# Loading the values of pairs 5 to 8 through GpSimd's software DMA queue, in bf16

## The chip, the cores and the metric

The kernel runs on one core of a Trainium2 chip. Its engines work side by side, each in the order of its own queue: TensorE (PE, matrix products), VectorE (DVE), ScalarE (ACT), GpSimd (POOL) and SyncE (SP, which here only issues DMAs). Sixteen DMA engines carry data between HBM and the on-chip memories, whoever issued the transfer. The metric is the device time of one execution in microseconds (us), lower being better.

## What is computed

A gated linear attention with a complex decay, then a normalised feed-forward layer. Cut to what matters:

```python
# q, k, v, a_re, a_im: (4 batches, 8 heads, 768 steps, 48)
for t in range(S):
    S_re, S_im = ar * S_re - ai * S_im, ar * S_im + ai * S_re   # a, capped at |a| = 0.999
    S_re = S_re + outer(k[:, :, t], v[:, :, t])
    y[:, :, t] = q[:, :, t] @ S_re
x = y, heads side by side                                        # (4, 768, 384)
xn = (x - mean) / sqrt(var + 1e-6) * g_ln
out = x + relu(xn @ w_ch1) @ w_ch2                               # 384 -> 1536 -> 384
```

All inputs and the output are float32.

## The kernel before

The steps of time are cut into chunks of 128. Two chunks make a pair; a batch has three pairs, and the four batches give pairs 0 to 11 (so chunks 0 to 23, chunks 2P and 2P+1 being those of pair P). Per pair the kernel works out the running log magnitude and phase of the decay (`ln`, `iv`, `r`, `r2`, `u`, `l`, `lc`, `th` on the gates, `dec` and `ph` as matmuls with triangular matrices, then `e`, `en`, `sin`, `cos`), scales the keys and queries by them (`ke`, `qe`, then `ks`, `qs`, each with a cosine half `.0` and a sine half `.1`), and transposes these per chunk (`kT`/`ksT`, `qT`/`qsT`: by PE and a copy, or by a DMA transpose issued from SP). Per chunk n, `am.n` is the product of keys and queries, `atm.n` its masked copy, `gm.n` adds keys times values to the state, `G.n` copies the state out, `y.n` is `atm` times values plus queries times state, `x.n` its copy, `bn.n` its mean and variance, and `xtr`/`xT` its transpose. Per pair follow the feed-forward products `mm1`, `relu`, `mm2`, the scale `rstd`, the sum `ot` and the store `st`.

Nothing of the order is left to a scheduler. A long text, `PLAN`, lists every step as `name:engine`, with a digit for the PSUM bank. Each engine executes its steps in the order in which they stand there. A suffix `@other` makes a step wait until another has ended, which the author uses to let DVE and POOL take turns. Buffers are rings of a few tiles (`RINGS`): 2 for `vf`, 4 for `v`, 3 for `k`, `q`, `ks` and `qs`.

The change concerns the values. For each pair P, `vf.P.0` and `vf.P.1` (L403) load the two chunks as float32 from HBM into the tile `vf`, 128 partitions by 8 heads by 48 numbers each, issued by SP. `v.P` (L411 on ACT, L413 on DVE or POOL) then casts the whole pair, 128 x 768, to bf16 into the tile `v`, which the matmuls of `gm` (L643) and `y` (L665) read. The plan puts `v.5` on DVE, `v.6` and `v.8` on POOL and `v.7` on ACT. The weights are loaded by POOL's software queue (`wl`, L363 and L365), which casts them from float32 to bf16 on the way.

The loads issued from SP wait in SP's queue with the DMA transposes (L597), the loads of gates, keys and queries (L444, L403) and the stores (L760), in the plan's order.

Of the kernel before, what the change touches and what calls it, by code (L numbers as in the profile page):

```python
# [24 lines left out]
RINGS = {"are": 3, "aim": 3, "q": 3, "k": 3, "vf": 2, "v": 4, "w": 2, "r": 3, "r2": 2, "l": 3,  # L25
# [6 lines left out]


QUARTER = {0, 1, 2, 3}

ENGINES = {"P": "PE", "A": "ACT", "V": "DVE", "G": "POOL", "S": "SP"}

# [41 lines left out]
am.7:P2 r2.5.0:A xT.4:V7 q.5.0:S xtr.5:P0 decc.4:V6 am.6:P4 r.6.0:G ot.3:V1 xT.5:A0 ph.5.0:P6 cos.4.0:A  # L79
vf.4.1:S atm.6:V4 mm1.2.1.1:P0 sin.5.0:A6 are.7.0:S ke.4.0.0:G atm.7:V2 y.6:P4 mm1.2.1.0:P0 abs.5.0:A6  # L80
ke.4.0.1:G gm.6:P5 x.6:A4 are.8.0:S mm1.2.2.0:P2 G.6:V5 cos.5.0:A qe.4.0.1:G xtr.6:P4 relu.2.1:V0 y.7:P6
gm.7:P5 q.5.1:S ks.4.0.1:G x.7:A6 mm1.2.2.1:P2 bn.4:V r2.6.0:A xtr.7:P0 mm1.2.0.1:P6 vf.5.0:S xT.7:V0
relu.2.2:A2 xT.6:V4 mm1.2.0.0:P6 qs.4.0.0:G G.7:V5 st.1:S th.6.0:A bn.7:V mm1.3.0.0:P0 k.5.0:S relu.2.0:V6
mm1.3.1.0:P2 ks.4.0.0:G aim.7.0:S mm1.3.2.1:P4 bn.5:V mm1.3.2.0:P4 tab.log.8:A u.5.0:A bn.6:V rstd.2:G
mm1.3.1.1:P2 u.6.0:A qs.4.0.1:V mm2.5.0:P6 l.5.0:V relu.3.2:A4 qsT.9:S mm2.4.0:P7 mm1.3.0.1:P0 lc.5.0:V
relu.3.1:A2 l.6.0:V ksT.8:S mm2.4.1:P7 ln.7.0:A relu.3.0:V0 dec.5.0:P4 vf.5.1:S mm2.4.2:P7 e.5.0:A4 q.6.1:S
lc.6.0:V v.4:V mm2.5.1:P6 en.5.0:A4 st.3:S qe.5.0.1:V dec.6.0:P2 ot.4:V7 k.5.1:S iv.7.0:A mm2.6.0:P0 en.6.0:A2
r.7.0:G k.6.1:S qT.8:P1 kT.9:P7 ln.8.0:A qsT.8:V1 mm2.5.2:P6 aim.8.0:S e.6.0:A2 ksT.9:V7 am.8:P4 qe.5.0.0:G
r2.7.0:A mm2.7.0:P1 atm.8:V4 st.4:S gm.8:P7 rstd.3:A qs.5.0.0:G st.2:S am.9:P2 u.7.0:A G.8:V7 aim.9.0:S
mm2.6.1:P0 atm.9:V2 ph.6.0:P4 ke.5.0.0:G k.6.0:S qs.5.0.1:V y.9:P2 tab.trig.9:A th.7.0:A gm.9:P7 l.7.0:V  # L90
y.8:P3 q.6.0:S mm2.7.1:P1 abs.6.0:A4 x.9:V2 ke.5.0.1:G@l.7.0 mm2.6.2:P0 are.9.0:S car.6.0:A4 G.9:V7 sin.6.0:A4
mm2.7.2:P1 x.8:V3 qe.6.0.1:V oa.6:A0 qT.11:P7 vf.6.0:S bn.8:V xtr.8:P2 xtr.9:P3 ph.7.0:P4 lc.7.0:V xT.9:A3
q.7.1:S xT.8:V2 cos.6.0:A ks.5.0.0:V mm1.4.1.1:P2 abs.7.0:V4 vf.6.1:S ke.6.0.1:G@ks.5.0.0 car.7.0:A4
mm1.4.1.0:P2 sin.7.0:A4 ks.5.0.1:V dps.6:P0 qsT.10:S oa.7:A1 v.5:V mm1.4.0.1:P4 relu.4.1:A2 ke.6.0.0:V
mm1.4.0.0:P4 qsT.11:V7 ot.6:G@ke.6.0.0 k.7.1:S kT.11:P1 relu.4.0:V4 mm1.4.2.0:P2 ks.6.0.0:G k.7.0:S
mm1.4.2.1:P2 decc.6:V0 tab.log.10:A ln.9.0:A ksT.11:V1 mm2.8.0:P7 q.7.0:S relu.4.2:A2 ot.5:V6 qe.6.0.0:G
kT.10:P0 bn.9:V am.11:P4 k.8.1:S iv.8.0:A qs.6.0.0:G mm2.9.0:P6 ksT.10:V0 rstd.4:A st.6:S dec.7.0:P2 atm.11:V4
# [2 lines left out]
th.9.0:A y.11:P1 kT.12:P2 ke.7.0.1:G th.8.0:A x.11:V1 q.8.0:S y.10:P3 qsT.13:V0 ksT.12:A2 xtr.11:P1 ks.7.0.1:G  # L100
ph.8.0:P4 x.10:V3 cos.7.0:A xT.11:V1 xtr.10:P0 ph.9.0:P2 abs.8.0:V4 xT.10:A0 ks.7.0.0:G ot.8:V7 mm1.5.0.1:P0
sin.9.0:A2 ot.9:V6 st.8:S mm1.5.0.0:P0 car.9.0:A2 q.8.1:S abs.9.0:V2 ot.7:G sin.8.0:A4 mm1.5.1.0:P6 are.10.0:S
relu.5.0:V0 vf.7.0:S mm1.5.1.1:P6 r2.8.0:A qe.7.0.1:G mm1.5.2.1:P2 cos.8.0:A qe.7.0.0:G are.11.0:S relu.5.1:V6
am.12:P4 r2.9.0:A mm1.5.2.0:P2 v.6:G atm.12:V4 st.9:S am.13:P0 qs.7.0.0:G vf.7.1:S mm2.10.0:P6 atm.13:V0
mm2.11.0:P7 tab.log.12:A u.8.0:A st.7:S y.12:P4 qs.7.0.1:G gm.12:P5 aim.10.0:S x.12:V4 mm2.10.1:P6 G.12:A5
bn.10:V relu.5.2:A2 mm2.11.1:P7 l.8.0:V ksT.15:S y.13:P0 u.9.0:A mm2.10.2:P6 lc.8.0:V x.13:A0 xtr.12:P1
bn.11:V gm.13:P5 k.9.1:S xT.12:A1 dec.8.0:P2 l.9.0:V rstd.5:G xtr.13:P0 dps.7:P4 en.8.0:A2 ksT.14:S
mm2.11.2:P7 xT.13:V0 G.13:V5 e.8.0:A2 ke.8.0.0:G@l.9.0 mm1.6.0.1:P0 ot.11:V7 ln.11.0:A vf.8.0:S mm1.6.2.1:P2
lc.9.0:V decc.7:V4 ln.10.0:A ke.8.0.1:G@lc.9.0 mm1.6.2.0:P2 vf.8.1:S v.7:A mm1.6.1.0:P4 ks.8.0.0:V aim.11.0:S
qT.15:P7 iv.10.0:A qe.8.0.1:G@ks.8.0.0 mm1.6.0.0:P0 qsT.15:V7 relu.6.2:A2 qe.8.0.0:G mm1.6.1.1:P4 ot.10:V6  # L110
vf.9.0:S relu.6.0:A0 gm.14:P7 bn.12:V r.10.0:G am.15:P2 k.9.0:S qT.14:P6 relu.6.1:A4 atm.15:V2 mm2.12.0:P0
qsT.14:A6 mm2.13.0:P1 qs.8.0.1:V dec.9.0:P4 G.14:V7 r2.10.0:V am.14:P2 qs.8.0.0:V mm2.12.1:P0 u.10.0:A
# [1 line left out]
gm.15:P7 ksT.17:S x.14:V2 xtr.15:P6 qT.16:P3 e.9.0:A4 G.15:V7 ke.9.0.1:G xtr.14:P2 mm2.13.2:P1 r.11.0:V  # L114
xT.14:A2 q.9.0:S mm2.12.2:P0 rstd.6:G xT.15:A6 ksT.16:S mm1.7.0.0:P4 ke.9.0.0:G@r.11.0 ot.12:V0 mm1.7.0.1:P4
qsT.16:V3 st.12:S tab.trig.13:A cos.9.0:A mm1.7.1.1:P6 st.11:S bn.15:V q.9.1:S mm1.7.2.0:P2 th.10.0:A l.10.0:V
vf.9.1:S mm1.7.2.1:P2 relu.7.0:A4 lc.10.0:V st.10:S mm1.7.1.0:P6 bn.14:V v.8:G@lc.10.0 relu.7.2:A2 k.10.0:S
dps.9:P0 ks.9.0.1:V mm2.15.0:P4 relu.7.1:A6 q.10.0:S decc.9:V0 am.17:P2 qe.9.0.0:V gm.16:P0 r2.11.0:A
atm.17:V2 ks.9.0.0:G@qe.9.0.0 q.10.1:S am.16:P6 mm2.15.1:P4 th.11.0:A G.16:V0 mm2.14.0:P5 atm.16:V6 v.9:G
ksT.18:S dec.10.0:P2 qe.9.0.1:G y.17:P0 ot.13:V1 tab.log.14:A u.11.0:A y.16:P6 k.11.0:S x.17:V0 mm2.14.1:P5  # L120
# [32 lines left out]
class Graph:  # L153
# [59 lines left out]
def kernel(  # L213
# [54 lines left out]
    def T(name, i):  # L268
        return tiles[name][i % RINGS[name]]
# [69 lines left out]
    def c_mask():  # L339
# [11 lines left out]
          needs=["ue"])  # L351
    for i in range(RINGS["car"]):
        g.add(f"car0.{i}", lambda i=i: nc.gpsimd.memset(tiles["car"][i], WINDOW),
                  needs=["ue"])
# [7 lines left out]
    for i in range(NG):  # L362
        g.add(f"wl.{i}", lambda i=i: nc.gpsimd.dma_start(  # L363
            out=w1b[:, :, ts(i, 512)], in_=moe_w_ch1.rearrange("(dc p) j -> p dc j", p=C)[:, :, ts(i, 512)]))
        g.add(f"wl.{NG + i}", lambda i=i: nc.gpsimd.dma_start(  # L365
            out=w2b[:, ts(i, JG)], in_=moe_w_ch2.rearrange("(jc p) e -> p jc e", p=C)[:, ts(i, JG)]))
# [11 lines left out]
    for jb in range(NG):  # L378
# [7 lines left out]
        for ec in range(ND):  # L386
            g.add(f"wc.{jb}.{ec}", lambda jb=jb, ec=ec, o=o: nc.vector.scalar_tensor_tensor(
                out=w1b[:, ec, ts(jb, 512)], in0=w1b[:, ec, ts(jb, 512)], scalar=gln[:, ds(ec, 1)],
# [3 lines left out]
    def pair_ops(P):  # L392
        b, pp = divmod(P, PB)
# [5 lines left out]
        add = g.add  # L399

        for c in range(R):
            for nm, ap in (("k", k), ("q", q), ("vf", v)):
                add(f"{nm}.{P}.{c}", lambda nm=nm, ap=ap, c=c: nc.sync.dma_start(  # L403
                    out=T(nm, P)[:, c],
                    in_=ap[b].rearrange("h (c p) d -> p c h d", p=C)[:, pp * R + c]),
                    uses=[(nm, P)])

        def f_v():
# [3 lines left out]
            else:  # L412
                {"DVE": nc.vector, "POOL": nc.gpsimd}[eng(nm)].tensor_scalar(  # L413
                    out=T("v", P), in0=T("vf", P), scalar1=1.0, scalar2=0.0, op0=ALU.mult,
                    op1=ALU.add)
        add(f"v.{P}", f_v, needs=[f"vf.{P}.0", f"vf.{P}.1"], uses=[("vf", P), ("v", P)])


        for i in range(NS):
# [23 lines left out]
            for nm, ap in (("are", a_re), ("aim", a_im)):  # L443
                add(f"{nm}.{X}", lambda nm=nm, ap=ap, hs=hs: nc.sync.dma_start(  # L444
                    out=T(nm, P)[:, hs], in_=ap[b][hs].rearrange(
                        "h (k p j) d -> p k h (j d)", p=C, j=R)[:, pp]), uses=[(nm, P)])
            add(f"ln.{X}", lambda S_=S_: act(out=S_("w"), in_=S_("are"), func=AF.Ln),  # L447
                needs=[f"are.{X}"], uses=[("are", P), ("w", P)])
            add(f"iv.{X}", lambda S_=S_: act(out=S_("are"), in_=S_("w"), func=AF.Exp, scale=-1.0),  # L449
                needs=[f"ln.{X}"], uses=[("are", P), ("w", P)])  # L450
            add(f"r.{X}", lambda S_=S_, X=X: tt(f"r.{X}", out=S_("r"), in0=S_("aim"), in1=S_("are"),
                                                op=ALU.mult),
                needs=[f"iv.{X}", f"aim.{X}"], uses=[("are", P), ("aim", P), ("r", P)])

            def f_r2(S_=S_, X=X):
# [6 lines left out]
                needs=[f"r2.{X}", "one"], uses=[("r2", P)])  # L462

            def f_l(S_=S_):
# [4 lines left out]
                out=S_("l"), in0=S_("l"), scalar1=LNCAP, scalar2=LNEPS, op0=ALU.min, op1=ALU.add),  # L469
                needs=[f"l.{X}"], uses=[("l", P)])  # L470
# [8 lines left out]
            for nm, sc in (("en", -1.0), ("e", 1.0)):  # L479
                add(f"{nm}.{X}", lambda nm=nm, sc=sc, X=X, fs=fs, view=view: act(  # L480
                    out=T(nm, P)[:, :, fs], in_=view(f"dec.{X}"), func=AF.Exp, scale=sc),
                    needs=[f"dec.{X}"], uses=[(nm, P)], ps=(f"dec.{X}", nb))

            add(f"th.{X}", lambda S_=S_: act(out=S_("th"), in_=S_("r"), func=AF.Arctan),
                needs=[f"r.{X}"], uses=[("r", P), ("th", P)])

            def f_ph(X=X, fs=fs, view=view, step=step):
# [12 lines left out]
                uses=[("th", P), ("car", P)], ps=(f"ph.{X}", nb))  # L500

            if not last:
                def f_car(X=X, fs=fs, v16=v16):
# [7 lines left out]
                    uses=[("car", P + 1)], ps=(f"ph.{X}", nb))  # L511
# [3 lines left out]
                needs=[f"ph.{X}"], uses=[("trig", P)], ps=(f"ph.{X}", nb))  # L515
# [48 lines left out]
        def stack(nm):  # L564
            return [f"{nm}.{P}.{i}.{a}" for i in range(NS) for a in range(2)]
# [19 lines left out]
        for c in range(R):  # L585
# [49 lines left out]
            if not (last and c == R - 1):  # L635
                def f_gm(n, c, nfirst):
                    ps = bank(f"gm.{P}")[:, 0:DM]
                    if c == 0 and not nfirst:
                        nc.tensor.matmul(ps, lhsT=ident,
                                         rhs=T("G", n - 1).rearrange("p h d -> p (h d)"),  # L640
                                         start=True, stop=True, skip_group_check=True)
                    for h in range(H):
                        nc.tensor.matmul(heads(ps)[:, h], lhsT=T("ks", P)[:, c, h],  # L643
                                         rhs=T("v", P)[:, c, h], start=nfirst, stop=True,
                                         skip_group_check=True)
                was = [] if nfirst else [f"G.{n - 1}"]
                add(f"gm.{n}", lambda n=n, c=c, nfirst=nfirst: f_gm(n, c, nfirst),
                    needs=stack("ks") + [f"v.{P}", f"pad.ks.{P % RINGS['ks']}"] + was,
                    uses=[("ks", P), ("v", P)] + ([("G", n - 1)] if was and c == 0 else []),
                    ps=(f"gm.{P}", 1))  # L650
                if c == 0:
                    add(f"G.{n}", lambda n=n: put(f"G.{n}", T("G", n),
                                                  heads(bank(f"gm.{P}")[:, 0:DM])),
                        needs=[f"gm.{n}"], uses=[("G", n)], ps=(f"gm.{P}", 1))
                else:
                    add(f"G.{n}", lambda n=n: tt(
                        f"G.{n}", out=T("G", n), in0=heads(bank(f"gm.{P}")[:, 0:DM]),
                        in1=T("dec", P).unsqueeze(2).to_broadcast([C, H, D]), op=ALU.mult),
                        needs=[f"gm.{n}", f"decc.{P}"], uses=[("G", n), ("dec", P)],
                        ps=(f"gm.{P}", 1))  # L660

            def f_y(n, c, nfirst):
# [143 lines left out]
```

## Time and profile before

The kernel took 193.36 us, the median of three runs (191.88, 193.36, 194.04). The profiled execution took 192.54 us, of which the profile's span is 190.8.

| what | value |
|---|---|
| PE busy | 174.8 us (92%), 2061 matmuls |
| DVE, ACT busy | 154.8 us (81%), 157.3 us (82%) |
| POOL busy | 109.9 us (58%), without its DMA issues |
| hardware DMA queue (SP) | 126960 packets, 34.09 MB, 86.2% of 16 engines |
| software DMA queue (POOL) | 2784 packets, 2.36 MB, 8.3% of 16 engines |
| loads of `vf` | 24 of 192 KB, median 4.2 us from issue to landing (3.3 to 10.9) |
| casts `v` | 7 on POOL (median 834 ns), 4 on DVE (552 ns), 1 on ACT (830 ns) |

Times in views of the trace are microseconds from the span's start. A line of the timeline gives the start, the time, the engine, the source line, the operation with output and input tiles, the count, and in square brackets how long the engine stood idle before it and what ended that. DMA packets here are runs of contiguous bytes: a chunk of values has 128 x 8 runs of 48 float32 numbers, 192 B each. The share of a queue can add up to more than 100% with others, since packets of several transfers are under way in one engine at once.

### The profile page before, as it was taken

To read this page: it belongs to the slowest core of one execution; us is meant where nothing else is said; L and a number is where in the kernel's file an instruction comes from. 1 tells how busy PE (TensorE), PEld (TensorE's weight loads), DVE (VectorE), ACT (ScalarE), POOL (GpSimd) and SP (SyncE) were. 2 spreads that over 40 slices of the span, in tenths; PEclk is the share of its full clock that TensorE was granted. 3 is DMA by queue.
4 is the path that set the end of the run, shared out by engine and by line. 5 is a ranking of instruction groups with operands and counts; after the bars stand their busy time and mean duration, and the time that the engine had idled before them with its cause. 6 is when DMAs were issued, how large, how long until landed. Compare 5 with 4: busy or idle time off the path is not lost.

```text
span 190.8 us, 5173 instructions
## 1 busy us (share of the span) xinstructions
PE 174.8 (92%) x2061; PEld 134.5 (70%) x2061; DVE 154.8 (81%) x283; ACT 157.3 (82%) x217; POOL 109.9 (58%) x128
## 2 busy tenths in 40 slices
PE   5758777999999999999899999999999999999990
PEld 4646455986868889676687786877768777886760
DVE  0397879998979999969979899798998898596422
ACT  4798998999898999999799898979996976283450
POOL 7505297599508999175291995758292756630030
PEclk9978999999999999999999999999999999999998
DMA  5999999899999999699989999987999999995132
GB/s 140 290 226 220 204 207 192 204 193 200 203 240 201 228 236 219 115 221 255 246 147 240 150 241 272 188 190 144 227 205 145 185 186 172 239 121 164 45 124 84
DMA packets 129768, 36.78 MB, mean 193 GB/s; under 512 B 123984, under 2 KB 129744, under 8 KB 129744
## 3 DMA queue, kind: packets, MB, share of 16 engines
q1 hardware_dynamic: 126960, 34.09, 86.2%
q0 software_dynamic: 2784, 2.36, 8.3%
q8 instruction: 16, 0.26, 0.6%
q14 instruction: 8, 0.07, 0.1%
HBM read 28.31 MB, written 4.72 MB: 173 GB/s over the span
## 4 chain that ended last, share of the span: by engine, by line
PE 50%; DMA 15%; DVE 9%; ACT 6%; POOL 6%; SPq 6%; issue 4%; POOLq 0%; DVEq 0%; ACTq 0%
PE banks L740 17%; PE banks L719 14%; DMA aim<-in_a_im_dram 5%; DMA w2b<-in_moe_w_ch_dram 4%; PE banks L592 4%; SPq L403 3%; PE banks L615 3%; PE banks L495 3%; DMA are<-in_a_re_dram 2%; PE banks L476 2%; DMA qsT<-qs 2%; DVE atm L291 2%; DMA q<-in_q_dram 2%; POOL r L291 2%; PE banks L665 2%
## 5 line engine op out<-in xcount | busy, mean ns | idle before, releaser
L740 PE MATMUL banks<-w2b,h 128*128 128x384 bf16 x288 | 55.3, 326 | 0.3 <-DMA w2b<-in_moe_w_ch_dram 0.3
L719 PE MATMUL banks<-xT,w1b 128*128 128x256 bf16 x432 | 51.3, 273 | 0.9 <-ACT trig L513 0.9
L719 PEld LDWEIGHTS <-w1b 128*128 128x128 bf16 x432 | 41.4, 98 | 7.3 <-issue 0.8
L740 PEld LDWEIGHTS <-h 128*128 128x128 bf16 x288 | 25.8, 97 | 13.5 <-issue 0.4
L291 DVE TENSOR_TENSOR atm<-banks,mask 128x1024 bf16<-128x1024 f32 x24 | 28.8, 1218 | 3.6 <-PE banks L615 3.5
L730 ACT ACTIVATE h<-banks 128x1024 bf16<-128x1024 f32 x26 | 26.0, 1019 | 5.7 <-PE banks L719 4.4
L291 POOL TENSOR_TENSOR ke<-k,en 128x384 bf16<-128x384 f32 x19 | 17.2, 916 | 16.8 <-DVE qs L291 5.8
L774 ACT ACT_TABLE_LOAD x19 | 24.4, 1283 | 1.1 <-PEq L790 0.8
L291 POOL TENSOR_TENSOR ks<-ke,trig 128x768 bf16<-128x768 bf16 (+1 forms) x12 | 18.9, 1583 | 6.6 <-DVE qs L291 2.0
L752 POOL TENSOR_TENSOR ot<-ot,x 128x384 f32<-128x384 f32 x7 | 6.4, 916 | 18.2 <-ACT ot L745 15.9
L291 POOL TENSOR_TENSOR qs<-qe,trig 128x768 bf16<-128x768 bf16 (+1 forms) x10 | 15.7, 1569 | 0.3
L754 DVE SCALAR_TENSOR_TENSOR ot<-banks,rstd,x 128x384 f32<-128x384 f32 x17 | 10.3, 610 | 6.8 <-ACT h L730 3.5
L615 PE MATMUL banks<-qsT,ksT 128*128 128x128 bf16 x192 | 14.6, 219 | 1.1 <-DVE ksT L288 0.9
L291 POOL TENSOR_TENSOR qe<-q,e 128x384 bf16<-128x384 f32 x14 | 12.7, 918 | 4.2 <-ACT trig L513 3.4
L615 PEld LDWEIGHTS <-ksT 128*128 128x128 bf16 x192 | 12.0, 98 | 3.2 <-DVE ksT L288 1.0
L291 POOL TENSOR_TENSOR r<-aim,are 128x768 f16<-128x768 f32 x6 | 10.9, 1816 | 5.5 <-ACT are L449 5.4
L476 PE MATMUL banks<-l,u_e 128*128 128x384 f16 (+1 forms) x52 | 10.9, 342 | 3.5 <-DVE l L468 3.4
L732 DVE TENSOR_SCALAR h<-banks 128x1024 bf16<-128x1024 f32 x10 | 12.1, 1216 | 2.0 <-PE banks L719 2.0
L678 DVE BATCH_NORM_STATS2 stats<-x 128x6 f32<-128x384 bf16 x24 | 13.1, 547 | 0.0
L769 PE MATMUL banks<-u_e 128*128 128x256 f16 x72 | 11.1, 312 | 2.2 <-POOL u_e L325 2.2
L447 ACT ACTIVATE w<-are 128x768 f32<-128x768 f32 (+1 forms) x13 | 10.1, 794 | 3.4 <-DMA are<-in_a_re_dram 3.3
L665 PE MATMUL banks<-v,atm 128*128 128x48 bf16 x192 | 12.1, 183 | 0.1
(95 smaller groups left out, 383.7 us busy)
## 6 DMA issues: line engine op xcount, KB each, us to landing
k<-in_k_dram SPq DMA_DIRECT2D x24, 192.0 KB, 4.0
q<-in_q_dram SPq DMA_DIRECT2D x24, 192.0 KB, 4.3
vf<-in_v_dram SPq DMA_DIRECT2D x24, 192.0 KB, 4.2
out_dram<-ot SPq DMA_DIRECT2D x24, 192.0 KB, 2.9
are<-in_a_re_dram SPq DMA_DIRECT2D x11, 384.0 KB, 4.6
aim<-in_a_im_dram SPq DMA_DIRECT2D x11, 384.0 KB, 5.0
w1b<-in_moe_w_ch_dram POOLq DMA_DIRECT2D x3, 384.0 KB, 7.0
w2b<-in_moe_w_ch_dram POOLq DMA_DIRECT2D x3, 384.0 KB, 7.7
```

The source lines that it names most:

```text
L291: {"DVE": nc.vector, "POOL": nc.gpsimd}[eng(name)].tensor_tensor(**kw)
L476: nc.tensor.matmul(heads(ps[:, c]), lhsT=u_e[:, c, j], rhs=step(T("l", P), j), start=(j == 0), stop=(j == R - 1))
L615: nc.tensor.matmul(ps[:, h], lhsT=T("ksT", n)[:, h], rhs=T("qsT", n)[:, h], start=True, stop=True)
L665: nc.tensor.matmul(ps[:, h], lhsT=T("atm", n)[:, h], rhs=T("v", P)[:, c, h], start=True, stop=nfirst)
L678: nc.vector.bn_stats(out=T("stats", n), in_=T("x", n))
L719: nc.tensor.matmul(ps[:, jj], lhsT=w1b[:, dc, ts(gi * JG + jj, C)], rhs=T("xT", P)[:, dc].rearrange("p c t -> p (c t)"), start=(dc == 0), ...
L730: act(out=dst, in_=src, func=AF.Relu)
L732: nc.vector.tensor_scalar(out=dst, in0=src, scalar1=0.0, scalar2=None, op0=ALU.max)
L740: nc.tensor.matmul(bank(f"o.{n}")[:, 0:DM], lhsT=T("h", P)[:, j, ts(c, C)], rhs=w2b[:, j], start=(j == 0), stop=(j == NJ - 1))
L754: nc.vector.scalar_tensor_tensor(out=T("ot", n), in0=bank(f"o.{n}")[:, 0:DM], scalar=T("rstd", P)[:, ds(c, 1)], in1=T("x", n), op0=ALU.mul ...
L769: g.add(f"warm.{i}", lambda i=i: nc.tensor.matmul(bank(f"warm.{i}")[:, 0:256], lhsT=u_e[:, 0, 0], rhs=u_e[:, 1].rearrange("p j t -> p (j t ...
L774: g.add(f"tab.{nm}.{i}", lambda tab=tab: nc.scalar.preload_act_table_set(tab))
```

## The change

For pairs 5 to 8 the loads of the values are issued by POOL instead of SP. They write straight into the bf16 tile `v`; the DMA converts. The casts `v.5` to `v.8` go, and so does these pairs' use of `vf`. In the plan each `vf.P.c` keeps its place in the text, with the engine changed from S to G, so that it now stands in POOL's queue between the POOL steps that surround it there. The matmuls of `gm` and `y` wait for the two loads instead of the cast.

```diff
+CAST = {5, 6, 7, 8}
...
             for nm, ap in (("k", k), ("q", q), ("vf", v)):
+                if nm == "vf" and P in CAST:
+                    add(f"vf.{P}.{c}", lambda c=c: nc.gpsimd.dma_start(
+                        out=T("v", P)[:, c],
+                        in_=v[b].rearrange("h (c p) d -> p c h d", p=C)[:, pp * R + c]),
+                        uses=[("v", P)])
+                    continue
                 add(f"{nm}.{P}.{c}", lambda nm=nm, ap=ap, c=c: nc.sync.dma_start(
...
-        add(f"v.{P}", f_v, needs=[f"vf.{P}.0", f"vf.{P}.1"], uses=[("vf", P), ("v", P)])
+        if P not in CAST:
+            add(f"v.{P}", f_v, needs=[f"vf.{P}.0", f"vf.{P}.1"], uses=[("vf", P), ("v", P)])
+        values = [f"v.{P}"] if P not in CAST else [f"vf.{P}.{c}" for c in range(R)]
...
-                    needs=stack("ks") + [f"v.{P}", f"pad.ks.{P % RINGS['ks']}"] + was,
+                    needs=stack("ks") + values + [f"pad.ks.{P % RINGS['ks']}"] + was,
...
-                needs=[f"atm.{n}", f"v.{P}"] + ([] if nfirst else [f"G.{n - 1}", f"qsT.{n}"]),
+                needs=[f"atm.{n}"] + values + ([] if nfirst else [f"G.{n - 1}", f"qsT.{n}"]),
```

In the plan, `vf.5.0` to `vf.8.1` change from `:S` to `:G`, and `v.5:V`, `v.6:G`, `v.7:A` and `v.8:G@lc.10.0` are taken out. POOL's queue around the new issues then reads as follows (an excerpt, POOL's steps alone):

```
ks.4.0.1  vf.5.0  qs.4.0.0  ks.4.0.0  rstd.2  vf.5.1  r.7.0
ke.5.0.1@l.7.0  vf.6.0  vf.6.1  ke.6.0.1@ks.5.0.0
ot.7  vf.7.0  qe.7.0.1  qe.7.0.0  qs.7.0.0  vf.7.1  qs.7.0.1  rstd.5
ke.8.0.0@l.9.0  vf.8.0  ke.8.0.1@lc.9.0  vf.8.1  qe.8.0.1@ks.8.0.0  qe.8.0.0  r.10.0
```

More of the change, by code (lines that the diff above doesn't have):

```diff
@@ L81 @@
 ke.4.0.1:G gm.6:P5 x.6:A4 are.8.0:S mm1.2.2.0:P2 G.6:V5 cos.5.0:A qe.4.0.1:G xtr.6:P4 relu.2.1:V0 y.7:P6
-gm.7:P5 q.5.1:S ks.4.0.1:G x.7:A6 mm1.2.2.1:P2 bn.4:V r2.6.0:A xtr.7:P0 mm1.2.0.1:P6 vf.5.0:S xT.7:V0
+gm.7:P5 q.5.1:S ks.4.0.1:G x.7:A6 mm1.2.2.1:P2 bn.4:V r2.6.0:A xtr.7:P0 mm1.2.0.1:P6 vf.5.0:G xT.7:V0
 relu.2.2:A2 xT.6:V4 mm1.2.0.0:P6 qs.4.0.0:G G.7:V5 st.1:S th.6.0:A bn.7:V mm1.3.0.0:P0 k.5.0:S relu.2.0:V6
@@ L85 @@
 mm1.3.1.1:P2 u.6.0:A qs.4.0.1:V mm2.5.0:P6 l.5.0:V relu.3.2:A4 qsT.9:S mm2.4.0:P7 mm1.3.0.1:P0 lc.5.0:V
-relu.3.1:A2 l.6.0:V ksT.8:S mm2.4.1:P7 ln.7.0:A relu.3.0:V0 dec.5.0:P4 vf.5.1:S mm2.4.2:P7 e.5.0:A4 q.6.1:S
+relu.3.1:A2 l.6.0:V ksT.8:S mm2.4.1:P7 ln.7.0:A relu.3.0:V0 dec.5.0:P4 vf.5.1:G mm2.4.2:P7 e.5.0:A4 q.6.1:S
 lc.6.0:V v.4:V mm2.5.1:P6 en.5.0:A4 st.3:S qe.5.0.1:V dec.6.0:P2 ot.4:V7 k.5.1:S iv.7.0:A mm2.6.0:P0 en.6.0:A2
@@ L91 @@
 y.8:P3 q.6.0:S mm2.7.1:P1 abs.6.0:A4 x.9:V2 ke.5.0.1:G@l.7.0 mm2.6.2:P0 are.9.0:S car.6.0:A4 G.9:V7 sin.6.0:A4
-mm2.7.2:P1 x.8:V3 qe.6.0.1:V oa.6:A0 qT.11:P7 vf.6.0:S bn.8:V xtr.8:P2 xtr.9:P3 ph.7.0:P4 lc.7.0:V xT.9:A3
-q.7.1:S xT.8:V2 cos.6.0:A ks.5.0.0:V mm1.4.1.1:P2 abs.7.0:V4 vf.6.1:S ke.6.0.1:G@ks.5.0.0 car.7.0:A4
-mm1.4.1.0:P2 sin.7.0:A4 ks.5.0.1:V dps.6:P0 qsT.10:S oa.7:A1 v.5:V mm1.4.0.1:P4 relu.4.1:A2 ke.6.0.0:V
+mm2.7.2:P1 x.8:V3 qe.6.0.1:V oa.6:A0 qT.11:P7 vf.6.0:G bn.8:V xtr.8:P2 xtr.9:P3 ph.7.0:P4 lc.7.0:V xT.9:A3
+q.7.1:S xT.8:V2 cos.6.0:A ks.5.0.0:V mm1.4.1.1:P2 abs.7.0:V4 vf.6.1:G ke.6.0.1:G@ks.5.0.0 car.7.0:A4
+mm1.4.1.0:P2 sin.7.0:A4 ks.5.0.1:V dps.6:P0 qsT.10:S oa.7:A1
+mm1.4.0.1:P4 relu.4.1:A2 ke.6.0.0:V
 mm1.4.0.0:P4 qsT.11:V7 ot.6:G@ke.6.0.0 k.7.1:S kT.11:P1 relu.4.0:V4 mm1.4.2.0:P2 ks.6.0.0:G k.7.0:S
@@ L102 @@
 sin.9.0:A2 ot.9:V6 st.8:S mm1.5.0.0:P0 car.9.0:A2 q.8.1:S abs.9.0:V2 ot.7:G sin.8.0:A4 mm1.5.1.0:P6 are.10.0:S
-relu.5.0:V0 vf.7.0:S mm1.5.1.1:P6 r2.8.0:A qe.7.0.1:G mm1.5.2.1:P2 cos.8.0:A qe.7.0.0:G are.11.0:S relu.5.1:V6
-am.12:P4 r2.9.0:A mm1.5.2.0:P2 v.6:G atm.12:V4 st.9:S am.13:P0 qs.7.0.0:G vf.7.1:S mm2.10.0:P6 atm.13:V0
+relu.5.0:V0 vf.7.0:G mm1.5.1.1:P6 r2.8.0:A qe.7.0.1:G mm1.5.2.1:P2 cos.8.0:A qe.7.0.0:G are.11.0:S relu.5.1:V6
+am.12:P4 r2.9.0:A mm1.5.2.0:P2
+atm.12:V4 st.9:S am.13:P0 qs.7.0.0:G vf.7.1:G mm2.10.0:P6 atm.13:V0
 mm2.11.0:P7 tab.log.12:A u.8.0:A st.7:S y.12:P4 qs.7.0.1:G gm.12:P5 aim.10.0:S x.12:V4 mm2.10.1:P6 G.12:A5
@@ L107 @@
 bn.11:V gm.13:P5 k.9.1:S xT.12:A1 dec.8.0:P2 l.9.0:V rstd.5:G xtr.13:P0 dps.7:P4 en.8.0:A2 ksT.14:S
-mm2.11.2:P7 xT.13:V0 G.13:V5 e.8.0:A2 ke.8.0.0:G@l.9.0 mm1.6.0.1:P0 ot.11:V7 ln.11.0:A vf.8.0:S mm1.6.2.1:P2
-lc.9.0:V decc.7:V4 ln.10.0:A ke.8.0.1:G@lc.9.0 mm1.6.2.0:P2 vf.8.1:S v.7:A mm1.6.1.0:P4 ks.8.0.0:V aim.11.0:S
+mm2.11.2:P7 xT.13:V0 G.13:V5 e.8.0:A2 ke.8.0.0:G@l.9.0 mm1.6.0.1:P0 ot.11:V7 ln.11.0:A vf.8.0:G mm1.6.2.1:P2
+lc.9.0:V decc.7:V4 ln.10.0:A ke.8.0.1:G@lc.9.0 mm1.6.2.0:P2 vf.8.1:G
+mm1.6.1.0:P4 ks.8.0.0:V aim.11.0:S
 qT.15:P7 iv.10.0:A qe.8.0.1:G@ks.8.0.0 mm1.6.0.0:P0 qsT.15:V7 relu.6.2:A2 qe.8.0.0:G mm1.6.1.1:P4 ot.10:V6
@@ L116 @@
 qsT.16:V3 st.12:S tab.trig.13:A cos.9.0:A mm1.7.1.1:P6 st.11:S bn.15:V q.9.1:S mm1.7.2.0:P2 th.10.0:A l.10.0:V
-vf.9.1:S mm1.7.2.1:P2 relu.7.0:A4 lc.10.0:V st.10:S mm1.7.1.0:P6 bn.14:V v.8:G@lc.10.0 relu.7.2:A2 k.10.0:S
+vf.9.1:S mm1.7.2.1:P2 relu.7.0:A4 lc.10.0:V st.10:S mm1.7.1.0:P6 bn.14:V
+relu.7.2:A2 k.10.0:S
 dps.9:P0 ks.9.0.1:V mm2.15.0:P4 relu.7.1:A6 q.10.0:S decc.9:V0 am.17:P2 qe.9.0.0:V gm.16:P0 r2.11.0:A
```

## The prediction

> **What bounds the kernel now.** I read the busy table of the page first, then busy time by stretches, then TensorE's (PE's) instructions in order, then the queue that the change loads (GpSimd, POOL) with the vector engine (DVE) beside it. The page, engine by engine, in 40 slices of 4.77 us:
>
> ```profile
> PE   5758777999999999999899999999999999999990
> DVE  0397879998979999969979899798998898596422
> ACT  4798998999898999999799898979996976283450
> POOL 7505297599508999175291995758292756630030
> PEclk9978999999999999999999999999999999999998
> ```
>
> From slice 9 (43 us) to slice 36 PE is full and its granted clock is full; DVE and ScalarE (ACT) are nearly so. Busy time by stretches (columns: window, length, busy us and count of PE, PEld, DVE, ACT, POOL, clock, DMA share, GB/s), for those the change touches last:
>
> ```profile
> 104.00:116.00 12.00, 12.00 (x150) 9.50 (x148) 11.44 (x16) 11.45 (x16) 11.63 (x10) 1.00 1.10 211
> 116.00:128.00 12.00, 11.95 (x152) 9.49 (x151) 10.51 (x23) 10.26 (x15) 6.93 (x8) 1.00 1.18 218
> ```
>
> A busy PE could still be a waiting PE, so I looked at when its matmuls start:
>
> ```profile
> 119.44 2.78 PE L719 MATMUL banks<-xT,w1b 128*128 128x256 bf16 x24
> 122.06 0.61 PE L592 MATMUL banks<-ident,qs 128*128 128x128 bf16 x8
> 122.51 1.47 PE L719 MATMUL banks<-xT,w1b 128*128 128x256 bf16 x12
> 123.82 0.33 PE L639 MATMUL banks<-G,ident 128*128 128x384 bf16 x1
> 123.98 0.36 PE L643 MATMUL banks<-v,ks 128*128 128x48 bf16 x8
> ```
>
> 24 matmuls of 256 columns go from 119.44 to 122.06, 109 ns each; the 12 after 122.51 take 109 ns each again (1.31 / 12). In the same way 384 columns take 163 ns, 128 take 56, 48 take 25.5. Laying these prices over all start times, I find that from 69 us to 178 us PE has gaps of only about 3.2 us, the largest 0.9 us before 94.80 (ScalarE's sine), 0.5 before 137.91, 0.4 before 172.86. So PE is the bound and its order is fixed. That caps any gain near 3 us, while a value that comes late to PE costs its whole lateness. The change first moves an instruction at 69 us (vf.5.0 on SP), so nothing before that shifts.
>
> **The change part by part.** Names are those of the plan.
>
> Removed: four casts. v.5 on DVE (93.79, 0.55 us) has an idle DVE 1.6 us behind it (0.97 us, until PE's L719 at 96.38). v.7 on ACT (121.36, 0.83 us) stands in front of the wait of 1.11 us that ends at 127.68. v.8 on POOL (136.36) sat after a wait of 2.38 us, and the next POOL step waits for DVE's qe.9.0.0 until 138.62. Those three free no time on the path, except that DVE's ks.9.0.1 (136.88) lasted 0.72 us beside v.8, against 0.55 for the same operation at 91.79: -0.17. v.6 on POOL (112.01, spacing to the next 0.80 us) is a real saving in a full stretch, and is spent below. SP loses eight issues: 1.10 + 0.57 + 0.68 + 1.09 + 0.72 + 0.43 + 1.26 (two) = 5.85 us. SP is nearly full from 76 to 125 us but then stands 2.7 us (125.45 to 128.18) for DVE's qs of pair 8, and so returns to the old time; the transposes before that come at most a few us earlier, and PE has no gap there that ends on one. I take 0.
>
> Added: eight issues on POOL. The nearest rows are the weight loads on the same queue, also with a cast, and the steps around the last pair of issues:
>
> ```profile
> 36.36 0.81 POOL L365 DMA_DIRECT2D w2b<-in_moe_w_ch_dram  x1
> 37.20 1.48 POOL L291 TENSOR_TENSOR r<-r 128x768 f16<-128x768 f16 x1
> ...
> 119.89 0.92 POOL L291 TENSOR_TENSOR ke<-k,en 128x384 bf16<-128x384 f32 x1
> 121.10 0.92 POOL L291 TENSOR_TENSOR ke<-k,en 128x384 bf16<-128x384 f32 x1 [0.29 <-DMA ksT<-ks]
> 122.75 1.79 POOL L291 TENSOR_TENSOR qe<-q,e 128x384 bf16<-128x384 f32 x2 [0.73 <-ACT v L411]
> 124.49 1.81 POOL L291 TENSOR_TENSOR r<-aim,are 128x768 f16<-128x768 f32 x1
> ```
>
> POOL's next step starts at 37.20, so an issue holds POOL for s = 0.81 us. That load has 128 x 4 = 512 runs; w1b with 128 x 3 = 384 runs took 0.80 (23.97), two in a row 1.79. A load of v has 128 x 8 = 1,024 runs of 192 B. Three bounds: by bytes (a quarter) 0.2; flat 0.81; by runs 0.81 x 1,024/512 = 1.62 or 0.81 x 1,024/384 = 2.16. Since 384 and 512 runs cost the same I take 0.81 and keep 0.2 and 2.16. Place by place:
> - vf.5.0 before qs.4.0.0 (72.47), vf.5.1 after rstd.2 (76.82): POOL idles 5.42 us until 82.24, so 2s is hidden up to s = 2.7. The SP transposes behind it (76.90 on DVE's qs.4.0.1, then 78.34) want ks.4.0.0, done 75.7 + 0.8.
> - vf.6.0 and vf.6.1 after ke.5.0.1 (ends 89.81): the next step waits until 92.47; 1.62 of 2.66 us.
> - vf.7.0 before qe.7.0.1 (110.25), vf.7.1 before qs.7.0.1: +1.62 - 0.80 (v.6); qs.7.0.1 ends 116.86 for 116.04, and rstd.5 waits for DVE until 118.30. Hidden up to s = 1.5.
> - vf.8.0 between ke.8.0.0 (ends 120.81) and ke.8.0.1, vf.8.1 behind that: this pair has no cover. ke.8.0.1 starts at 121.62 for 121.10, +0.52. Who waits:
>
> ```profile
> 122.05 0.56 DVE L291 TENSOR_TENSOR ks<-ke,trig 128x768 bf16<-128x768 bf16 x1 [0.77 <-POOL ke L291]
> ...
> 124.90 1.23 DVE L291 TENSOR_TENSOR atm<-banks,mask 128x1024 bf16<-128x1024 f32 x1 [0.29 <-PE banks L615]
> ```
>
> DVE's ks.8.0.0 waits for that ke, with qsT.15, ot.10, bn.12 and atm.15 queued behind; before atm.15 DVE idled 0.29, so atm.15 is 0.52 - 0.29 = 0.23 late, and with it r2.10.0 (127.11), for which ACT waits until 127.68. r.10.0 on POOL ends at 120.81 + 2s + 0.92 + 1.79 + 1.81 = 126.95, just in time for 127.11. So +0.23.
>
> Moved: the transfers. A load on the software queue: w1b packets (2 KB of source) took 36.7% x 12 us x 16 / 687 = 103 ns in 12 to 24 us, w2b packets (1.5 KB) 68.8% x 10 x 16 / 1,329 = 83 ns in 36 to 46. The slope of 20 ns per 0.5 KB leaves 29 ns for 192 B; the hardware queue's took 84.5% x 12 x 16 / 7,855 = 21 ns at the start. So 1,024 x 29 / 16 = 1.9 us of all 16 DMA engines for 1.3, 0.5 us more per load; the upper bound is the unscaled 83 ns, 5.3 us. The values are awaited by PE alone: pair 5 at 101.5, 6 at 114.24, 7 at 123.98, 8 at 138.07. Their issues start at 78, 91, 114.5 and 122.5. Only pair 7 is near: 9.5 us, against 7.0 and 7.7 us from issue to landing for the weights (twice the bytes written) and 4.2 median, 10.9 at most for the loads of v now. Hidden, 0.
>
> Sum: +0.23 - 0.17 = about +0.1 us on the profiled execution, whose own time was 192.54 (span 190.8 and 1.7 around it), that is 192.6. The median of the three runs shown is 0.8 above it; so about 193.5, and I say 193.6, since more waits on POOL seldom meet as neatly as above.
>
> **The rivals.**
> 1. *Slower: the issue costs by its 1,024 runs.* The place is vf.8.0 in front of ke.8.0.1. With s = 1.62, r.10.0 ends at 128.7 and r2.10.0 is 1.6 late; with 2.16, rstd.5 is 1.26 late too, and r2.10.0 is 2 x 2.16 - 1.8 + 1.3 = 3.8 late: 195.0 to 197.2. It counts from s = 0.58 and passes 1% at about 1.7. For: 1,024 runs are not in the trace. Against: no slope from 384 to 512.
> 2. *Slower: the packets keep 83 ns.* Then each load holds the engines 4.0 us longer, 32 us over 70 to 130 us, where their share is already about 1; the transposes that PE needs (4.1 us to landing) would wait. A delay of one load for pairs 7 and 8 each gives +8, 201; for one alone 197.5.
> 3. *Slower: pair 7 lands late.* At 10.9 us after 114.5 it comes at 125.4, 1.4 us after PE's first use: 195.
> 4. *Slower: DVE shuts out the issue.* An issue that must wait out one DVE step of up to 1.2 us (atm) has s = 2.0, +3.1 by rival 1's sum: 196.6. Against it: the issue at 38.61 still took 0.81 with such a step beginning at 38.92. The Trainium skill (SBUF — State Buffer, "SBUF: two separate sides") states that descriptors of DMAs from GpSimd cannot be written while VectorE runs in a two-port mode; by that rule issues beside SBUF-to-SBUF DVE steps would stall, and the trace's six issues show no case of it.
> 5. *Faster: SP's freed 5.85 us reaches PE.* Loads and transposes come earlier and two thirds of PE's 3.2 us of gaps close: 191.2. Against: the gaps end on ACT and DVE, and only the one before 172.86 on a transpose.
>
> **How the numbers follow.** Forecast (within 1% of 193.36, which is what a measurement of this kernel can tell, its three runs spanning 1.1%): 0.53. Rival 1: 0.20, 2: 0.06, 3: 0.05, 4: 0.03, so slower 0.34. Rival 5: 0.13. The range goes from rival 5 (191.4) to the end of rival 1 (197.2) and leaves out most of rival 2 and the far side of 5. The forecast's own range is 192 to 195.
>
> **What would show it.** Right: POOL issues of v near 0.8 us; ke.8.0.1 half a us later against ke.8.0.0; no PE idle before L643 or L665 with the DMA of v as its end; PE starts as dense as before. Wrong: issues of 1.6 us and more with DVE waiting for POOL's ke; a wait of PE on in_v; landing of transposes well above 4.1 us; or PE gaps that shrink by 2 us.

## The result and the profile after

| | median | range, runs |
|---|---|---|
| before | 192.68 us | 191.52 to 194.04, 16 |
| after | 194.04 us | 193.08 to 195.28, 16 |

The ratio is 1.0071 (95% interval 1.0045 to 1.0097): some 1.4 us slower, within the 1% that was forecast, and clearly not nothing. The profiled execution of the changed kernel took 193.56 us, its span 191.4.

The page of the changed kernel, engine by engine and then its DMA queues:

```profile
PE   5758869999999999999899997998999999989991
...
POOL 7506296798438999495754995958193666530030
...
q1 hardware_dynamic: 118640, 32.52, 83.1%
q0 software_dynamic: 11104, 3.15, 16.4%
```

From 69 us on, where the change begins, PE is as full as before but for a 7 in the slice from 115 to 120 us and an 8 in those from 129 to 134 and from 167 to 172. POOL's digits, and its 109.9 us before, include its DMA issues: this page counts 134 instructions on POOL for 128 before, eight issues more and two casts fewer. The software queue has 8,320 more packets and 8.1 more points of 16 engines' span: 0.081 x 191.4 x 16 / 8,320 = 30 ns a packet.

The views of the tile `v` and of the DMA issues give the cost of an issue on POOL and the landing:

```profile
L411 POOL DMA_DIRECT2D v<-in_v_dram x8: 881/938/991, 70.9 to 122.3; - x8
```

```profile
v<-in_v_dram POOLq DMA_DIRECT2D x8, 96.0 KB, 5.5
ksT<-ks SPq DMA_TRANSPOSE x12, 4.8
qsT<-qs SPq DMA_TRANSPOSE x10, 4.0
```

An issue holds POOL for 0.94 us (0.88 to 0.99). Loads land after 4.2 to 7.4 us, 5.5 in the median, and no PE wait ends on one.

Where the time went is best read against an event that all runs share. PE's largest gap, before the L719 matmuls at 94.80 (93.47 after), ends on the same sine of ACT and is 0.86 us in both. From there to the first matmul of `gm.16`, the step that first reads pair 8's values, and from there to the last row of `mm2` matmuls:

| us | gap to gm.16 | gm.16 to the last mm2 |
|---|---|---|
| before | 94.80 to 137.91: 43.11 | to 183.08: 45.17 |
| after | 93.47 to 138.20: 44.73 | to 184.10: 45.90 |

The changed kernel loses 1.62 us in the first stretch (the profiled execution of before had merely arrived there 1.3 us later: it was 1.5 us behind at the same matmul near 60 us, ahead of the first step that the change moves). The 0.73 us of the second stretch come with a wait of 0.83 us before 169.28, for a copy on DVE, of which versions with the same loads below have 0.55 us, 0.32 or none (their second stretch takes 45.1 to 45.4 us); it is left open. What was lost stands in three places of DVE and POOL. In order of time, the two engines of the changed kernel (start, time, engine, line, operation):

```profile
111.72 1.64 POOL L298 TENSOR_TENSOR qs<-qe,trig 128x768 bf16<-128x768 bf16 x1
113.30 0.94 POOL L411 DMA_DIRECT2D v<-in_v_dram  x1
...
114.26 1.65 POOL L298 TENSOR_TENSOR qs<-qe,trig 128x768 bf16<-128x768 bf16 x1
114.78 0.18 DVE L694 BATCH_NORM_AGGREGATE mv<-stats 128x2 f32<-128x6 f32 x1
114.88 1.86 DVE L480 SCALAR_TENSOR_TENSOR l<-r,w 128x768 f16<-128x768 f16 x1
```

The same two steps before the change:

```profile
112.81 3.23 POOL L291 TENSOR_TENSOR qs<-qe,trig 128x768 bf16<-128x768 bf16 x2
...
116.21 0.93 DVE L465 SCALAR_TENSOR_TENSOR l<-r,w 128x768 f16<-128x768 f16 x1
```

`qs.7.0.1` ended at 116.04 and DVE's `l.8.0` began at 116.21: they just missed each other. With `vf.7.1` in front, `qs.7.0.1` runs from 114.26 to 115.91, `l.8.0` begins inside it and takes 1.86 us for 0.93. Taking its own 0.93 off its end (116.74) leaves 115.81, as if DVE had done nothing until POOL's step was all but over. `l.8.0` heads a chain (`lc.8.0`, `dec.8.0`) that PE waits for:

```profile
117.18 0.81 PE L491 MATMUL banks<-l,u_e 128*128 128x384 f16 x4 [0.99 <-DVE l L483]
```

The other two places, pair 8's issues (POOL) and DVE behind them:

```profile
120.38 0.98 POOL L411 DMA_DIRECT2D v<-in_v_dram  x1
121.39 0.93 POOL L298 TENSOR_TENSOR ke<-k,en 128x384 bf16<-128x384 f32 x1
122.25 0.94 POOL L411 DMA_DIRECT2D v<-in_v_dram  x1
123.21 1.79 POOL L298 TENSOR_TENSOR qe<-q,e 128x384 bf16<-128x384 f32 x2
124.97 1.80 POOL L298 TENSOR_TENSOR r<-aim,are 128x768 f16<-128x768 f32 x1
```

```profile
122.35 0.56 DVE L298 TENSOR_TENSOR ks<-ke,trig 128x768 bf16<-128x768 bf16 x1 [1.44 <-POOL ke L298]
...
125.90 1.30 DVE L298 TENSOR_TENSOR qs<-qe,trig 128x768 bf16<-128x768 bf16 x1
```

DVE waits 1.44 us for POOL's ke for 0.77 before, as forecast but for the longer issue. Then `qs.8.0.1` takes 1.30 us where it took 0.67: it begins at 125.90, and `r.10.0` on POOL runs until 126.77. Again, its end 127.20 less the 0.55 of such a step alone is 126.65, just before POOL's end.

### The profile page after: what moved, and what is told of

It is laid out like the page before. It is cut to its first block, busy times and chain, and to the rows that moved or that the text cites. A ratio compares the mean times of both kernels' runs of the same rounds, so it can differ in the third digit from the quotient of the medians.

```text
span 191.4 us, 5166 instructions
## 1 busy us (share of the span) xinstructions
PE 174.7 (91%) x2059; PEld 134.1 (70%) x2061; DVE 155.9 (81%) x282; ACT 156.4 (82%) x216; POOL 116.5 (61%) x134
## 4 chain that ended last, share of the span: by engine, by line
PE 55%; DVE 18%; DMA 8%; SPq 7%; ACT 4%; issue 3%; POOL 2%; DVEq 0%; POOLq 0%
PE banks L734 18%; PE banks L755 16%; DVE atm L298 5%; PE banks L607 5%; DMA w1b<-in_moe_w_ch_dram 4%; PE banks L630 3%; SPq L459 3%; PE banks L491 2%; PE banks L510 2%; DMA q<-in_q_dram 2%; DVE l L480 2%; SPq L416 2%; PE banks L680 2%; DMA aim<-in_a_im_dram 2%; SPq L612 2%
## 5 line engine op out<-in xcount | busy, mean ns | idle before, releaser
L480 DVE SCALAR_TENSOR_TENSOR l<-r,w 128x768 f16<-128x768 f16 (+1 forms) x13 | 12.3, 954 | 0.8 <-ACT r L476 0.7
L476 ACT ACTIVATE r<-r,one_b 128x768 f16<-128x768 f16 (+1 forms) x13 | 11.2, 881 | 2.2 <-DVE r L298 2.0
```

What stands on the lines that cost most here:

```text
L480: nc.vector.scalar_tensor_tensor(out=S_("l"), in0=S_("r2"), scalar=0.5, in1=S_("w"), op0=ALU.mult, op1=ALU.add)
```

## The experiments

Two theories stood against each other. Theory A: the loss is made by the order on POOL alone. The issues push POOL's steps back, so that they meet DVE's at a port of the on-chip memory that both use, and make DVE wait for `ke.8.0.1`. Theory B: the loss is in the transfers, whose packets in the software queue hold the DMA engines for 30 ns and not 21, and delay the DMA transposes.

**The issues in idle time** (`e1_slots` in the expectations below). The same loads, moved in POOL's queue alone:

```diff
-... ot.7 vf.7.0 qe.7.0.1 qe.7.0.0 qs.7.0.0 vf.7.1 qs.7.0.1
+... qs.6.0.0 vf.7.0 vf.7.1 ke.7.0.0 ... ot.7 qe.7.0.1 qe.7.0.0 qs.7.0.0 qs.7.0.1
-ke.8.0.0 vf.8.0 ke.8.0.1 vf.8.1 qe.8.0.1 qe.8.0.0 r.10.0
+ke.8.0.0 ke.8.0.1 qe.8.0.1 qe.8.0.0 r.10.0 vf.8.0 vf.8.1
```

> The changed kernel with its four last issues moved within GpSimd's queue into idle time: vf.7.0 and vf.7.1 behind qs.6.0.0 (before ke.7.0.0), vf.8.0 and vf.8.1 behind r.10.0. Transfers, sizes and queue are the same. Theory A (the 1.4 us lost come from GpSimd's order: the issues push GpSimd steps into VectorE's, at the port they share and where VectorE waits for ke.8.0.1): all of it comes back, and the casts that went give a little, ratio to the kernel before 0.996 to 1.000; l.8.0 takes 0.93 us, qs.8.0.1 0.55 to 0.7. Theory B (the software queue's packets hold the DMA engines longer, 30 ns for 21, and delay transposes): the same eight loads, so still near 1.007.

Measured: ratio to the kernel before 1.0007 (95% interval 0.9975 to 1.004). That is just above A's range, which the interval reaches, and clear of B's 1.007. The gap-to-`gm.16` stretch is 42.94 us (94.05 to 136.99). With this order the three steps of DVE read

```profile
115.46 0.93 DVE L480 SCALAR_TENSOR_TENSOR l<-r,w 128x768 f16<-128x768 f16 x1
...
121.33 0.56 DVE L298 TENSOR_TENSOR ks<-ke,trig 128x768 bf16<-128x768 bf16 x1 [0.77 <-POOL ke L298]
...
125.30 0.70 DVE L298 TENSOR_TENSOR qs<-qe,trig 128x768 bf16<-128x768 bf16 x1
```

0.93, 0.77 and 0.70 us, for 0.93, 0.77 and 0.67 before. The transfers are those of the changed kernel, some of them at other times, so B makes no part of the loss that can be seen; nor does PE's wait before 117.18 or the one before 129.79 in the changed kernel end on a transfer. That the stretch is 0.17 us shorter than before fits the step beside `v.8`, `ks.9.0.1`, which took 0.53 for 0.72.

**One exchange** (`e2_swap7`). `vf.7.1` behind `qs.7.0.1`, nothing else:

```diff
-qs.7.0.0 vf.7.1 qs.7.0.1
+qs.7.0.0 qs.7.0.1 vf.7.1
```

> The changed kernel with vf.7.1 and qs.7.0.1 exchanged on GpSimd, nothing else. Theory A: qs.7.0.1 ends about 0.9 us earlier, l.8.0 on VectorE goes from 1.86 us back to 0.93, and the kernel gains about 0.9 us: ratio to before 1.001 to 1.004. Theory B: 1.007.

Measured: 1.0052 (1.0023 to 1.0081). `l.8.0` is back at 0.93 us and the stretch is 43.79 us, 0.94 less than in the changed kernel, as A wants. The ratio is above A's range, and its interval holds B's 1.007 as well, so it does not decide; the gain over the changed kernel is read from the trace.

**Pair 8 alone.** `vf.8.0` and `vf.8.1` behind `r.10.0`, with pair 7 as changed:

> The changed kernel with vf.8.0 and vf.8.1 alone moved behind r.10.0. Theory A: l.8.0 still takes 1.86 us, but ks.8.0.0 no longer waits longer than before for ke.8.0.1 (0.8 us for 1.4) and qs.8.0.1 takes 0.55 to 0.7 us for 1.30: ratio to before 1.003 to 1.005. Theory B: 1.007.

Measured: 1.0038 (1.0013 to 1.0063), in A's range. `l.8.0` takes 1.86 us, the wait before `ks.8.0.0` is 0.77, `qs.8.0.1` takes 0.70, and the stretch is 43.88 us.

The two parts add up. Against the version with both moved (42.94), the changed kernel is longer by 1.79 us; pair 7's place alone makes 43.88 - 42.94 = 0.94, pair 8's place alone 43.79 - 42.94 = 0.85.

**The delay without the DMA.** In the kernel before, one POOL memset (it fills a spare tile with zeros) stands in front of `qs.7.0.1`:

```diff
+    g.add("hold", lambda: nc.gpsimd.memset(spare, 0.0))      # spare: 128 x 900 fp16
-... qs.7.0.0:G ... qs.7.0.1:G
+... qs.7.0.0:G ... hold:G qs.7.0.1:G
```

> The kernel before, with one GpSimd memset of a spare tile (128 x 900 fp16, some 0.93 us) in front of qs.7.0.1; all DMAs and casts as before. Theory A: l.8.0 meets qs.7.0.1 at the shared port and takes 1.8 us, TensorE gets a gap of about 1 us before the matmuls of dec.8.0, and the kernel loses 0.7 to 1.0 us: ratio 1.0035 to 1.005. Theory B: 1.000, as no transfer is touched.

Measured: 1.0041 (1.0013 to 1.0068). The memset took 0.84 us and not 0.93, so `qs.7.0.1` overlapped less of `l.8.0`:

```profile
114.70 0.84 POOL L345 MEMSET spare<- 128x900 f16 x1
115.51 1.63 POOL L291 TENSOR_TENSOR qs<-qe,trig 128x768 bf16<-128x768 bf16 x1
```

```profile
116.55 1.41 DVE L467 SCALAR_TENSOR_TENSOR l<-r,w 128x768 f16<-128x768 f16 x1
```

`l.8.0` ends at 117.96; less 0.93 this is 117.03, and POOL's step ended at 117.14. No transfer was touched, so this shows the collision by itself. In the trace it costs about half of what pair 7's issues cost: PE's gap before `dec.8.0` is 0.54 us where 1 us was expected, and the stretch is 43.59 us, 0.48 more than before, which is what `l.8.0` grew by. The ratio lies in A's range and clear of 1; the rest of its 0.8 us is in neither stretch of this trace, and its interval reaches down to 0.25 us. The Trainium skill (SBUF — State Buffer, "Who interferes with whom") says that a VectorE instruction with two SBUF inputs contends with a GpSimd instruction that reads SBUF (the on-chip memory that the tiles lie in), and that whoever comes second is blocked for the whole instruction; `l.8.0` and `qs.8.0.1` have two such inputs, and in the five overlaps above (1.86, 1.86, 1.30, 1.28 and 1.41 us in four kernels) DVE's own work began some 0.1 us before POOL's step ended. The trace agrees.

**Pairs 5 and 6 alone.** `CAST = {5, 6}`; pairs 7 and 8 as before.

> The changed kernel with pairs 5 and 6 alone in CAST: pairs 7 and 8 load through SP and are cast on ACT and GpSimd as before. Theory A: the four issues left stand in idle time of GpSimd, nothing on the path moves: ratio to before 0.999 to 1.002. Theory B (transfers): half of the loads, so half of the loss, 1.0035.

Measured: 0.9975 (0.9945 to 1.0006), stretch 43.13 us. The ratio is below A's range, which the interval reaches, and clear of B's 1.0035. These four issues cost nothing; the interval only just holds 1, so a small gain is neither shown nor excluded. It is the lowest ratio of all versions, but its interval overlaps that of the version with idle places.

**The two issues of pair 8.** The version with idle places, with `vf.8.0` back in front of `ke.8.0.1`:

> As e1_slots, but vf.8.0 back between ke.8.0.0 and ke.8.0.1; vf.8.1 stays behind r.10.0. It separates the two issues of pair 8. Theory A with the whole cost in the late ke.8.0.1: ks.8.0.0 waits 1.4 us, qe.8 and r.10.0 shift with it, qs.8.0.1 meets r.10.0 and takes over 1 us: ratio to before 1.002 to 1.005, like e2_swap7. If vf.8.1 in front of qe.8.0.1 makes the collision, qs.8.0.1 takes 0.7 us and the ratio is 1.000 to 1.002.

Measured: 1.001 (0.9979 to 1.0041), which tells nothing apart, since the interval reaches both ranges. The trace does: `ks.8.0.0` waits 1.45 us, `qs.8.0.1` takes 1.11 us, the stretch is 43.62 us, so 0.68 of pair 8's 0.85 us come with `vf.8.0` alone.

**What an issue costs.** The version with idle places, with pair 5's loads in two issues each and `vf.7.0` in four, in a single run:

> As e1_slots, with each load of pair 5 issued as two of 512 runs, and vf.7.0 as four of 256 runs. One look, for the time that an issue holds GpSimd: flat cost, 0.9 us whatever the runs; fixed part with a slope through 512 runs 0.81 and 1,024 runs 0.94 us: 0.74 to 0.75 for 256; in proportion to the runs, 0.47 for 512 and 0.23 for 256.

POOL's queue in this kernel (one row may be several issues):

```profile
72.34 1.59 POOL L412 DMA_DIRECT2D v<-in_v_dram  x2
...
89.86 1.82 POOL L412 DMA_DIRECT2D v<-in_v_dram  x2
99.73 3.82 POOL L412 DMA_DIRECT2D v<-in_v_dram  x5
```

Two issues of 512 runs take 1.59 us, 0.80 each; two of 1,024 take 1.82, 0.91 each; the last row is four of 256 and one of 1,024, so (3.82 - 0.94) / 4 = 0.72. That is nearest to the second of the three expectations: a line through these has a fixed part of about 0.65 us and some 0.3 ns a run. A quarter of the runs is three quarters of the price.

**More pairs** (`e7_more`). The version with idle places, with pairs 9, 10 and 11 on the software queue too: four issues in a row behind `ke.9.0.0`, two behind `qs.9.0.0`.

> As e1_slots, with pairs 9, 10 and 11 in CAST too: vf.9 and vf.10 issued behind ke.9.0.0 and vf.11 behind qs.9.0.0, where GpSimd idles 4.5 and 3.4 us. It takes casts off VectorE (v.10, v.11) and GpSimd (v.9) and six more issues from SP. Theory A: no order is disturbed and the VectorE casts near 157 and 168 us, which stood on the chain, are gone: ratio to before 0.993 to 0.999. Theory B: 14 loads on the software queue, 1.010 or more.

Measured: 1.0313 (1.0259 to 1.0366). This is a miss of theory A, and by far: 6 us, in the range that theory B gave. The profiled execution was the longest of the six (199.97 us), so the 6 us are not divided up from it; that PE waits 3.7 us for one transpose, and what SP does ahead of it, can be seen in it:

```profile
135.44 3.69 POOL L411 DMA_DIRECT2D v<-in_v_dram  x4
```

```profile
138.49 4.29 SPq L416 DMA_DIRECT2D q<-in_q_dram  x2
142.89 4.29 SPq L612 DMA_TRANSPOSE ksT<-ks  x1
...
147.85 4.03 SPq L612 DMA_TRANSPOSE ksT<-ks  x1
```

Each of the two transposes holds SP for over 4 us, while loads of the software queue are under way (the last of the four landed 9.0 us after its issue); before the change the same two took 1.71 and 1.93. `qsT.18`, queued behind them, is issued at 152.06, 5.6 us after DVE had finished the last of its inputs (146.43); before, that was 0.2 us (145.28 after 145.12). The transfers do matter, then, once enough of them stand beside transfers that are needed soon.

**The same loads at two places.** Only pair 11 added to the version with idle places, its two issues behind `ke.9.0.0` in one kernel (`e9_free`) and behind `qs.9.0.0` in the other.

> As e1_slots, with pair 11 in CAST too, its two issues behind ke.9.0.0 (GpSimd idle from 134 us; no DMA transpose is issued between 134 and 139). Theory C (a DMA transpose that SP issues while loads of the software queue are under way holds SP some 4 us for 1.3 to 1.9, and that is what cost e7_more its 6 us): no transpose meets these loads, ratio to before 0.996 to 1.002. Theory D (any load of pairs 9 to 11 on the software queue costs, wherever it stands, or the end of the kernel has no room for the earlier data): 1.005 or more.

> The same kernel as e9_free but with the two issues of pair 11 behind qs.9.0.0, at 144 us, among the four transposes of pair 9 (139 to 148 us). Same transfers, same number of them. Theory C: at least one of these transposes holds SP for 4 us, qsT.18 and qsT.19 come 2 to 4 us late, TensorE waits for them: ratio to before 1.008 to 1.02. If it was the row of four loads in e7_more that did it, and not the neighbourhood of transposes: 0.996 to 1.002, as e9_free.

Measured: 1.0052 (1.0019 to 1.0086) and 1.0042 (1.001 to 1.0074). Theory C missed both: the free place costs, and the place beside the transposes costs no more. Theory D, by which such a load costs wherever it stands, gave 1.005 or more; the first ratio is in that range, the second just under it. In both the stretch to `gm.16` is untouched (42.95 us) and the loss comes after it: 46.75 and 46.41 us from `gm.16` to the last `mm2`, for 45.32 without pair 11. Beside the transposes PE waits for one of them:

```profile
150.48 0.61 PE L630 MATMUL banks<-qsT,ksT 128*128 128x128 bf16 x8 [1.01 <-DMA qsT<-qs]
```

It was not held on SP, as theory C had it: the first of the two `qsT` that SP issues there took the usual 1.23 us, but landed 6.0 us after its issue, for 4.2 without pair 11. At the free place, with no transpose near, PE waits for DVE's `x`, which was late because DVE's `ot.13` before it had stood for a store:

```profile
143.73 0.34 PE L701 MATMUL banks<-ident,x 128*128 128x128 bf16 x3 [1.19 <-DVE x L295]
```

```profile
142.13 0.62 DVE L769 SCALAR_TENSOR_TENSOR ot<-banks,rstd,x 128x384 f32<-128x384 f32 x1 [1.52 <-DMA out_dram<-ot]
```

`ot.13` writes the buffer that the store `st.10` empties. SP issued that store at 135.42, 1 to 2 us after pair 11's loads, and it landed after 6.7 us, for 4.1 without pair 11. An ordinary load beside it, `vf.9.1`, landed after 6.9 us for 4.3; POOL's cast waited 2.15 us for it, and `qs.9.0.0`, pushed back by that, met `l.11.0` on DVE (1.63 us for 0.95): the collision of pair 7 once more, this time set off by a transfer.

So there was no free place at 134 us: what SP issues beside two loads of the software queue lands later, and it costs if that is wanted at once. How the 6 us of the kernel with all three pairs divide among transposes, stores, ordinary loads and the row of four was not settled.

## Why the prediction was right

The median of 194.04 lies in the forecast's own range of 192 to 195 and 0.4 us from the value given; the direction, a small loss, was right too. By its steps:

- *What bounds the kernel* held: from 69 us on PE never waits more than 1 us at a time, and what the first stretch lost appears in the main as PE gaps in the two places where DVE was late (0.99 us before 117.18 and 0.59 before 129.79, for 0.2 and 0.1 between the same matmuls before).
- *The casts that went* gave what was said: nothing on the path, and 0.17 us from `ks.9.0.1`; the stretch of the version with idle places is shorter by just that. SP's 5.85 us came to nothing, as taken.
- *The issue*, taken flat at 0.81 us, is 0.94 us; it grows with the runs, but slowly. Rival 1 had the place of pair 8 right, but its prices by runs (1.62, 2.16) fall.
- *The places.* Pairs 5 and 6 cost nothing (0.9975, with 1 inside the interval). For pair 7 the step said that the push of `qs.7.0.1` is hidden until `rstd.5`, up to s = 1.5. This is the step that failed: it looked at who waits for POOL's result, not at what DVE does meanwhile. The push of some 1 us put `qs.7.0.1` on top of `l.8.0`, +0.94 us. For pair 8 the late `ke.8.0.1` was foreseen and priced at +0.23; it is +0.85, since the wait is 0.67 longer for the 0.52 worked out, and since `r.10.0`, priced as just in time, meets `qs.8.0.1` at the port.
- *The sum* was therefore +0.1 where +1.4 was measured. The value given was 0.9 above the median of the sixteen runs of before, 192.68, since it was set against the first three runs (193.36). Set against these sixteen, the sum gives 192.8, which is 1.3 below the measured median. So the range and "within 1%" were right, the loss was priced at less than a tenth of its size, and the nearness of the value is luck.
- *The transfers*: 30 ns a packet for the 29 worked out (the slope as written leaves 30.5), so rival 2's 83 ns is gone; landing 5.5 us, so rival 3 is gone. That they are hidden held for these eight loads, and did not hold for more. Rival 5's gain from SP's freed time did not come either: the version with idle places, which frees the same time, has a ratio of 1.0007.
- *Rival 4* had the port right and the direction wrong: no issue was held up by DVE (0.88 to 0.99 us), while POOL steps that the issues pushed held up DVE. The rule that it quotes speaks of two-port modes alone; which of DVE's steps ran in one is not shown here, so these issues do not test it.
- Two slips of the working changed nothing: with s = 1.62 `r.10.0` ends at 128.57 by its own terms, not 128.7, and rival 5 stands at 191.2 in its text and at 191.4 in the range.

## What to carry to other kernels

When a step is put in an engine's queue, price not only who waits for the steps behind it, but whom they will now run beside: two engines that share a port can lose a whole instruction to a shift of a microsecond, with no semaphore to show it; the sign here was a DVE step that took 1.5 to 2.4 times its usual time and whose usual time, counted back from its end, began just before its neighbour on POOL ended. An idle stretch of the queue is worth more than the place where the old step stood: the same eight issues cost 1.4 us or nothing. And the transfers that are moved to another queue still meet those that stay: look at what lands late beside them, stores included, as a store that frees a buffer can hold up the chain.

## What was not expected of the hardware

A DMA transpose issued while loads of the software queue are under way can hold SP for 4 us and more. In the kernel before, a single one takes 1.2 to 2.8 us from 69 us on. In the changed kernel the `qsT` at 90.63, issued while pair 6's loads were under way, takes 4.08 for 2.75, and in the other versions with these loads 3.6 to 5.9; it did no harm there: no PE wait ends on it, and the version with idle places has it too (4.26). The Trainium skill (DMA: Bandwidth & Descriptors, "Issuing engines are not separate DMA queues") states that DMAs of all issuing engines end on the same sixteen DMA engines and interleave there; the late `qsT`, store and `vf.9.1` of the last two kernels agree with it. And a software issue of 128 x 8 runs of 192 B holds GpSimd for 0.94 us, of which some 0.65 do not depend on the number of runs, an estimate from the issues of 256, 512 and 1,024 runs.
